# Crossbar transposes, pooled banks for the PV sums, and half of VectorE's exponent products on GpSimd, in a fused attention and feed-forward kernel

## The chip, the cores and the metric

One core of a Trainium2 chip runs the whole kernel. Times are device microseconds (us) of one execution, as the median of several; lower is better.

## The reference

```python
x = A_x                                        # (1, 2048, 512) bf16, 32 heads of 16
h  = x + attention(layernorm(x), wqkv, wo)     # softmax(q k^T / 4) v, no mask
h2 = h + (gelu(ln(h) @ w_gate) * (ln(h) @ w_up)) @ w_down     # F = 1792; returned
```

The costly part is 32 heads x 2048 x 2048 exponentials: 2048 score tiles of 128 keys by 512 queries, with one column of ones beside V so that the PV product yields the softmax's denominators too (PV: the exponentials times V). The queries are taken in five chunks of 512, 512, 512, 256 and 256 tokens.

## The kernel before

The program is laid out at build time. Small generators offer operations; a list scheduler with durations of its own puts them in a fixed order on each engine. On the chip each engine runs its order and waits on semaphores. So **how many** score tiles go to VectorE instead of ScalarE is a result of the scheduler.

TensorE writes score tiles to PSUM banks 0 to 3 for ScalarE, two at a time, and single tiles to other banks for VectorE. ScalarE's share is one instruction per pair:

```python
yield Op("act", TEXP(n), ACTF(PT[:, p0:p0 + n, :], pbank[:, b0:b0 + n, :], ACT.Exp, ...))    # 128x1024
```

VectorE's share is one conversion per tile (`dconv`, PSUM to 16-bit integers) and, for four tiles at once, two bitwise steps and a product, which split 2^x into two factors:

```python
def dchain(G):                       # X, W, E: (128, 4*512), 16 bit
    yield Op("dve", t1, ... out=W, in0=X, scalar1=0x3ff,  scalar2=0xb800, op0=bitwise_and, op1=bitwise_or)
    yield Op("dve", t1, ... out=E, in0=X, scalar1=0x7c00, scalar2=0x8,    op0=bitwise_and, op1=bitwise_or)
    yield Op("dve", t2, lambda e: e.tensor_tensor(out=X.bitcast(F16), in0=W, in1=X.bitcast(F16), op=ALU.mult), ...)
```

The PV sums of all heads gather in one bank (`PVB = 4`); when a unit of four heads by 512 queries is full it is copied out, transposed on TensorE and scaled:

```python
def ofin(u):
    yield Op("dve", 0.6, lambda e: e.tensor_copy(out=OA[:, par, :], in_=pbank[:, PVB, :]), ...)
    b = yield Acquire(...)                                   # another bank for the transposed sums
    yield Op("pe", 4 * TTR, fns=[TR(pt[:, ...], OA[:, par, ...], ident) for qt in range(4)], ...)
    ... reciprocal and the scalings, on VectorE, read from that bank
```

Padding is there to keep TensorE's clock up: where TensorE's order has a hole, the scheduler puts in a matmul of zeros, 512 columns wide (`fill_op`).

Of the kernel before, what the change touches and what calls it, by code (L numbers as in the profile page):

```python
# [165 lines left out]
ALU = mybir.AluOpType  # L166
# [694 lines left out]
class Op:  # L861
    def __init__(self, eng, dur, fns, reads=(), writes=(), gate=None, then=None, dma=None, extra=None, cols=0, port=False, mode="f"):
        self.eng, self.dur, self.cols, self.mode = eng, dur, cols, mode
        self.fns = fns if isinstance(fns, list) else [fns]
        self.reads, self.writes = list(reads), list(writes)
        self.gate, self.then, self.dma, self.extra = gate, then, dma, extra
        self.port = port or eng == "pool"


class Acquire:  # L870
    def __init__(self, reads=(), gate=None):
        self.reads, self.gate = list(reads), gate
# [15 lines left out]
class Sched:  # L888
# [5 lines left out]
    def __init__(self, P, banks):  # L894
        self.P = P
        self.t = {n: 0.0 for n in P.ENGINES}
        self.done = {}
        self.streams = []
        self.banks = [(0.0, b) for b in banks]
        self.now = 0.0  # L900
        self.fill = None
        self.debt = (0.0, 0.0)
        self.pipe = 0.0
        self.lent = set()
        self.early = True
        self.wake = None
        self.port = 0.0
        self.room = lambda: False
        self.mode = "f"
        self.due = self.INF  # L910
# [20 lines left out]
    def _rank(self, s):  # L931

        op = s.head
        if isinstance(op, Op):
            if s.fast is not None:
                return s.fast
            if op.eng == "pe" and op.writes[0] in SOFT:
                return min(s.prio, HELD[0] + s.prio * 1e-6) if self.room() else s.prio
            if op.eng == "dve" and not s.dyn and any(k in SOFT for k in op.reads):
# [3 lines left out]
    def _ready(self, op):  # L943
# [9 lines left out]
        if isinstance(op, Op):  # L953
# [5 lines left out]
            lag = SLACK if (op.eng == "pe" and op.writes[0] in SOFT) or (op.eng == "act" and op.writes[0][0] == "w") else 0.0  # L959
# [10 lines left out]
    def _emit(self, op, start):  # L970
# [7 lines left out]
        if op.eng == "pe":  # L978
            m = "r" if op.mode == "q" else op.mode
            if m != self.mode:  # L980
                start += TSW
            self.mode = m
        end = start + op.dur
        if op.port:
# [6 lines left out]
        else:  # L991
# [9 lines left out]
            self.done[tok] = end + TAIL.get(op.eng, 0.0)  # L1001
        if op.then is not None:
            op.then()

    def guard(self, cands):
# [5 lines left out]
        ok = [(r, s) for r, s in cands if s.head.mode == "q" or max(self.t["pe"], r) + s.head.dur + (TSW if s.head.mode[0] != self.mode else 0) <= due + QTOL]  # L1011
        return ok

    def run(self):
        while self.streams:
# [21 lines left out]
            for eng, cands in best.items():  # L1037
                if eng == "pe":
                    cands = self.guard(cands)
                st = max(self.t[eng], min(r for r, _ in cands))  # L1040
                lim = st + LOOK
                for r, s in cands:
                    if r <= lim:
                        st = max(self.t[eng], r)
# [22 lines left out]
            if op.eng == "pe" and self.fill:  # L1067
                f = self.fill(st, op)
                if f:
                    alt = [c for c in best["pe"] if c[1] is not s and c[0] <= f[1] + 0.05 and c[1].head.writes[0] in SOFT and c[1].head.cols >= 512]  # L1070
# [3 lines left out]
                    st, s = max(self.t["pe"], alt[0][0]), alt[0][1]  # L1074
# [9 lines left out]
SOFT = (("pb", 5), ("pb", 6), ("pb", 7))  # L1084
# [13 lines left out]
PVB = 4  # L1098
DENSE = (5, 6, 7)
# [4 lines left out]
GS = 4  # L1104
NX = 4
# [56 lines left out]
def fast_path(nc, P, base0, ARENA, pbank, flag, A_x, A_wqkv, A_wo, B_x, B_w_gate, B_w_up, B_w_down, out):  # L1162
# [20 lines left out]
    dW = at("dW", [128, GS, 512], F16)  # L1183
# [7 lines left out]
    xnT = at("xnT", [128, 4, S], BF16)  # L1191
# [4 lines left out]
    cur[0] = max(cur[0], offF + 43008)  # L1196
    dXE.append(at("dXE%d" % (NX - 1), [128, 2, GS, 512], U16, offE + 14336))
# [14 lines left out]
    hnT_c = [at("hnT_c%d" % c, [128, 4, CHUNKS[c]], BF16, h_off[c][0] + 4096) for c in range(NC)]  # L1212
# [47 lines left out]
    C = dict(exp=0, pv=0, oa=0, ln1=0, proj=0, oproj=0, gut=0, down=0, act=0, gopen=None, gk=0, gw=0, cdone=0, pvu=0, pvleft=0, gpv=0, acons=0, qpos=0, dnext=0.0, made=0)  # L1260
    otok_n = {}

# [49 lines left out]
    def masks():  # L1312
# [5 lines left out]
        yield Op("dve", 0.5, lambda e: e.memset(pbank[:, PVB, :], 0.0), writes=[("pb", PVB)])  # L1318
# [53 lines left out]

    def ln1_T(c, t):
        b = yield Acquire(reads=[("xn", t % 8), "ident"])
# [4 lines left out]
        o_ap, i_ap = xnT[:, :, 128 * t:128 * t + 128], pt[:, 0:512].rearrange("p (c s) -> p c s", c=4)  # L1379
# [5 lines left out]
    def proj_kq(items):  # L1385
        for (which, j, c, dl) in items:
# [4 lines left out]
            for hf in range(2):  # L1391
                yield Op("pe", 2 * TMM, cols=1024, fns=[MM(pbank[:, b, :], wqkv_sb[:, dc, base + 128 * j:base + 128 * j + 128], xnT[:, dc, 512 * c:512 * c + 512], dc == 0, dc == 3)
# [16 lines left out]
    def q_evac(j, c, b, dl):  # L1409

        for par in range(2):
# [8 lines left out]
    def proj_v():  # L1420
        for t in range(NT):
# [3 lines left out]
            for hf in range(2):  # L1425
                yield Op("pe", 2 * TMM, cols=1024, fns=[MM(pbank[:, b, :], xnT[:, dc, 128 * t:128 * t + 128], wqkv_sb[:, dc, 2 * D:3 * D], dc == 0, dc == 3)
# [39 lines left out]
    def qk():  # L1466
        nxt, an = 0, 0
        while nxt < len(TILES):
# [15 lines left out]
            yield Op("pe", TST * repeats([TILES[i][2] for i, _ in put]), mode="q", cols=128 * len(put), fns=fns, reads=rd, writes=[("pb", b) for _, b in put],  # L1484
# [14 lines left out]
    def close_group():  # L1499
        G = C["gopen"]  # L1500
        C["gopen"] = None
        if G["t"]:
            groups.setdefault(G["u"], []).append(G)
            sch.add(dchain(G), 70000).dyn = lambda: -4 if G["u"] == C["pvu"] and C["pvleft"] <= 5 else 70000
# [24 lines left out]
    def dget():  # L1529

        def room():
            if C["gopen"] or C["proj"] < DFROM or C["gw"] + 1 < C["gk"] or C["gk"] - C["gpv"] >= (NX if C["ln1"] == NT else NX - 1) or sch.t["dve"] > sch.now + 0.8:
# [5 lines left out]
        while True:  # L1538
            yield Wait(lambda: "qkdone" in C or room())
            if "qkdone" in C:  # L1540
                return
            G = C["gopen"] = dict(u=None, t=[], g=set(), k=C["gk"], conv=0)
            C["gk"] += 1
            C["dnext"] = sch.now + DGAP
            while len(G["t"]) < GS:
                if pick(G) is None:
                    if "qkdone" in C or (G["t"] and over(G)):
                        break
                    yield Wait(lambda: "qkdone" in C or pick(G) is not None or (G["t"] and over(G)))
                    continue  # L1550
                b = yield Acquire(gate=lambda: "qkdone" in C or over(G) or pick(G) is not None)
                i = pick(G)
                if i is None:
                    sch.release(b)
                    continue
                own[i] = ("d", G["k"])
                fns, rd = scores([(i, b)])
                wk = sch.wake | {TILES[i][2]}
                yield Op("pe", TDQ if TILES[i][2] not in sch.wake else TST, mode="r", cols=128, fns=fns, reads=rd, writes=[("pb", b)])
# [3 lines left out]
                G["g"].add(TILES[i][2])  # L1563
            close_group()

    def over(G):

        return bool(G["t"]) and unit0[G["u"] + 1] - C["qpos"] <= GLAST

    def pick(G):  # L1570
# [4 lines left out]
        if not G["t"]:  # L1575
            G["u"] = None
            u = unit_of(nxt)
            if unit0[u + 1] - nxt < ATAIL:
                u += 1
            if u < NU and qk_ready(u):  # L1580
                G["u"] = u
        u = G["u"]
        if u is None or not sch.wake or over(G):
            return None
        i0 = max(nxt, unit0[u])
        cand = [i for i in range(i0, min(unit0[u + 1], i0 + AWIN)) if i not in own and TILES[i][2] not in G["g"] | sch.wake]
        return cand[0] if cand else None

    def dconv(G, j, b):
        yield Op("dve", 0.603, lambda e: e.tensor_scalar(out=dXE[G["k"] % NX][:, 0, j, :], in0=pbank[:, b, :], scalar1=XMIN + 1024.0 * CENTER, scalar2=XMIN, op0=ALU.add, op1=ALU.max),  # L1590
                 reads=[("pb", b)], writes=[("dX", G["k"] % NX, j)], gate=lambda: C["gpv"] >= G["k"] - NX + 1 and (G["k"] % NX < NX - 1 or C["ln1"] == NT), extra=dE if G["k"] % NX == NX - 1 else None)
        sch.release(b)
        G["conv"] += 1

    def dchain(G):



        x, n = G["k"] % NX, len(G["t"])
        X, W, E = dXE[x][:, 0, 0:n, :], dW[:, 0:n, :], dXE[x][:, 1, 0:n, :]  # L1600
        kX, kW, kE = [("dX", x, j) for j in range(n)], ["dW"], [("dE", x)]
        t1, t2 = 0.07 + 0.133 * n, 0.066 + 0.267 * n
        yield Wait(lambda: G["conv"] == n)
# [3 lines left out]
        yield Op("dve", t2, lambda e: e.tensor_tensor(out=X.bitcast(F16), in0=W, in1=X.bitcast(F16), op=ALU.mult), reads=kW + kX, writes=kX, port=True)  # L1607
        G["done"] = 1

    def pv():  # L1610
        n = 0
        count = {}

        def total(u, g):
            return len(units[u][1]) * sum(2 if own[unit0[u] + 4 * kt + g][0] == "d" else 1 for kt in range(NT))

        def prod(i, tiles, last):

            u, kt, g = TILES[i]
            c, slots = units[u]  # L1620
            nq = CHUNKS[c]
            out = []
            for e, slot in enumerate(slots):
                for tl in tiles:
                    out.append((len(out), MM(pbank[32 * g:32 * g + 17, PVB, e * nq:e * nq + nq], VA[:, kt, head(slot, g), :], tl[:, e * nq:e * nq + nq],
                                             (u, g) not in count, last and count.get((u, g), 0) + 1 == total(u, g), (0, 32 * g))))
                    count[u, g] = count.get((u, g), 0) + 1
            return out

        for u in range(NU):  # L1630
            c, slots = units[u]
            r = len(slots)
            for m in range(0, NT, PVM):
                C["pvu"], C["pvleft"] = u, NT - m
                last = m + PVM >= NT
                ts = list(range(4 * n, 4 * (n + PVM)))
                yield Wait(lambda: all(i in own and (own[i][0] == "d" or i in made) for i in ts) and
                           (not last or ((not C["gopen"] or C["gopen"]["u"] != u or not C["gopen"]["t"]) and all("done" in G for G in groups.get(u, ())))))
                for G in groups.get(u, ()):
# [314 lines left out]
```

## Time and profile before

| | before |
|---|---|
| time, median of 3 | 845.17 us (844.28 to 845.54) |
| first exponential of ScalarE begins | 17.0 us |
| last one ends | 807.4 us |
| from there to the end (the tail) | 35.8 us |
| pairs of tiles on ScalarE | 796, busy 742.3 us |
| tiles on VectorE | 456, in 115 groups |

ScalarE's stage runs from its first exponential to its last. The lines behind the table, and the sum that they make, are in the prediction. The span is from the first to the last instruction; the time is some 2 us longer.

### The profile page before, as it was taken

What the parts mean: (1) busy time and instruction counts of PE and PEld (TensorE: products, weight loads), DVE (VectorE), ACT (ScalarE), POOL (GpSimd) and SP (SyncE); (2) the same over time, 40 slices, a digit from 0 to 9 for tenths busy, and PEclk for the clock granted to TensorE, in tenths of its full rate; (3) what the DMA queues carried; (4) which work ended last, traced back from release to release, by engine and by line L of the source; (5) the groups of instructions that cost most, each with busy time, mean ns of one, the idle gap of its engine ahead of it and who ended that gap; (6) DMA issues with size and microseconds to landing.
All of it is one profiled execution on the core that took longest, in us unless ns stands there. A gap on an engine that the chain in (4) does not pass through costs nothing.

```text
span 843.2 us, 16693 instructions
## 1 busy us (share of the span) xinstructions
PE 819.5 (97%) x6773; PEld 254.4 (30%) x6773; DVE 769.0 (91%) x1246; ACT 786.3 (93%) x833; POOL 42.9 (5%) x100
## 2 busy tenths in 40 slices
PE   8999999999999999999999989999999989999997
PEld 3222222222222222222222222222233333333455
DVE  7569999999999999999989989999999999899862
ACT  3979999999999999999999999999999999999941
POOL 5600000000010000000010000000010000000000
PEclk9999999999999999999999999999999999999999
DMA  6000004300000000000000000000000000000000
GB/s 200 1 1 1 1 2 160 116 1 1 8 7 1 2 1 2 7 26 7 2 14 1 1 1 2 7 26 7 2 21 7 2 1 2 2 26 14 2 13 18
DMA packets 12327, 15.06 MB, mean 18 GB/s; under 512 B 1744, under 2 KB 11216, under 8 KB 12240
## 3 DMA queue, kind: packets, MB, share of 16 engines
q1 hardware_dynamic: 12240, 13.90, 5.0%
q8 instruction: 55, 0.90, 0.4%
q14 instruction: 32, 0.26, 0.1%
HBM read 11.80 MB, written 2.10 MB: 16 GB/s over the span
## 4 chain that ended last, share of the span: by engine, by line
PE 75%; ACT 12%; DVE 6%; issue 5%; POOL 1%; ACTq 0%; POOLq 0%; DVEq 0%
PE pbank L1272 46%; PE pbank L1271 21%; ACT PT L1278 11%; PE pbank L1870 3%; DVE dXE L1590 2%; DVE dXE L1607 1%; PE pbank L1275 1%; ACT GUT L1809 1%; PE pbank L1867 1%; PE pbank L1880 1%; DVE dXE L1605 1%; POOL xn_sb L1369 1%; DVE dW L1604 1%; PE pbank L1725 0%; PE pbank L1747 0%
## 5 line engine op out<-in xcount | busy, mean ns | idle before, releaser
L1278 ACT ACTIVATE PT<-pbank 128x1024 bf16<-128x1024 f32 x796 | 742.3, 1072 | 17.7 <-PE pbank L1272 14.6
L1272 PE MATMUL pbank<-QT,KT 32*128 32x512 bf16 x2048 | 345.0, 384 | 7.2 <-ACT PT L1278 4.9
L1590 DVE TENSOR_SCALAR dXE<-pbank 128x512 uint16<-128x512 f32 x456 | 296.9, 682 | 15.9 <-PE pbank L1272 12.8
L1272 PEld LDWEIGHTS pbank<-QT,KT 32*128 32x128 bf16 x2048 | 84.2, 91 | 311.5 <-ACT PT L1278 220.8
L1272 PE MATMUL pbank<-PT,VA 128*17 128x512 bf16 (+1 forms) x1992 | 149.4, 339 | 0.1
L1607 DVE TENSOR_TENSOR dXE<-dW,dXE 128x2048 f16<-128x2048 f16 (+1 forms) x115 | 139.1, 1210 | 2.0
L1604 DVE TENSOR_SCALAR dW<-dXE 128x2048 uint16<-128x2048 uint16 (+1 forms) x115 | 78.1, 679 | 0.8
L1605 DVE TENSOR_SCALAR dXE<-dXE 128x2048 uint16<-128x2048 uint16 (+1 forms) x115 | 78.1, 679 | 0.0
L1272 PE MATMUL pbank<-dXE,VA 128*17 128x512 f16 (+1 forms) x1136 | 70.3, 339 | 0.0
L1271 PE MATMUL pbank<-hnT_c,wu_sb 128*128 128x512 bf16 (+1 forms) x280 | 59.7, 346 | 7.4 <-DVE GUT L1823 6.8
L1271 PE MATMUL pbank<-hnT_c,wg_sb 128*128 128x512 bf16 (+1 forms) x280 | 65.5, 340 | 0.0
L1271 PE MATMUL pbank<-wd_sb,GUT 128*128 128x512 bf16 x224 | 59.2, 382 | 0.0
L1272 PEld LDWEIGHTS pbank<-PT,VA 128*17 128x17 bf16 x1992 | 39.2, 88 | 65.3 <-issue 57.8
L1870 PE MATMUL pbank<-ones_bf,zero_bf 128*128 128x512 bf16 x168 | 55.7, 386 | 0.0
L1823 DVE TENSOR_TENSOR GUT<-pbank,GUT 128x512 bf16<-128x512 f32 x56 | 37.3, 685 | 16.0 <-PE pbank L1271 12.8
L1741 POOL TENSOR_SCALAR rstd<-mv 128x1 f32<-128x1 f32 x16 | 6.6, 413 | 761.0 <-DVE mv L1739 761.0
L1271 PE MATMUL pbank<-xnT,wqkv_sb 128*128 128x512 bf16 x128 | 37.8, 383 | 0.0
L1271 PEld LDWEIGHTS pbank<-hnT_c,wu_sb 128*128 128x128 bf16 x280 | 23.5, 99 | 32.5 <-issue 11.8
L1797 DVE CAST GUT<-pbank 128x512 bf16<-128x512 f32 x49 | 33.1, 680 | 0.0
L1271 PEld LDWEIGHTS pbank<-hnT_c,wg_sb 128*128 128x128 bf16 x280 | 19.5, 97 | 27.8 <-issue 20.6
L1272 PEld LDWEIGHTS pbank<-dXE,VA 128*17 128x17 bf16 x1136 | 18.7, 88 | 29.8 <-issue 24.0
L1271 PEld LDWEIGHTS pbank<-wd_sb,GUT 128*128 128x128 bf16 x224 | 17.0, 97 | 27.0 <-issue 14.3
(82 smaller groups left out, 390.8 us busy)
## 6 DMA issues: line engine op xcount, KB each, us to landing
xres<-in_A_x_dram SPq DMA_DIRECT2D x16, 128.0 KB, 2.2
out_dram<-out_sb SPq DMA_DIRECT2D x16, 128.0 KB, 1.7
wg_sb<-in_B_w_gate_dram SPq DMA_DIRECT2D x1, 1792.0 KB, 7.1
wu_sb<-in_B_w_up_dram SPq DMA_DIRECT2D x1, 1792.0 KB, 11.2
wd_sb<-in_B_w_down_dram SPq DMA_DIRECT2D x1, 1792.0 KB, 17.4
x_sb<-in_A_x_dram SPq DMA_DIRECT2D x3, 512.0 KB, 8.3
wqkv_sb<-in_A_wqkv_dram SPq DMA_DIRECT2D x1, 896.0 KB, 7.5
x_sb<-in_A_x_dram SPq DMA_DIRECT2D x2, 256.0 KB, 2.9
```

The source lines that it names most:

```text
L1271: return lambda e: e.matmul(o, l, r, start=start, stop=stop)
L1272: return lambda e: e.matmul(o, l, r, start=start, stop=stop, tile_position=tile)
L1275: return lambda e: e.transpose(out=o, in_=i, identity=idn)
L1278: return lambda e: e.activation(out=o, in_=i, func=func, **kw)
L1369: lambda e: e.tensor_scalar(out=xn_sb[:, t % 8, :], in0=x_sb[:, t, :], scalar1=rstd[:, tt_], scalar2=htmp[:, tt_], op0=ALU.mult, op1=ALU.add),
L1590: yield Op("dve", 0.603, lambda e: e.tensor_scalar(out=dXE[G["k"] % NX][:, 0, j, :], in0=pbank[:, b, :], scalar1=XMIN + 1024.0 * CENTER, s ...
L1604: yield Op("dve", t1, lambda e: e.tensor_scalar(out=W.bitcast(U16), in0=X, scalar1=0x3ff, scalar2=0xb800, op0=ALU.bitwise_and, op1=ALU.bit ...
L1605: yield Op("dve", t1, lambda e: e.tensor_scalar(out=E, in0=X, scalar1=0x7c00, scalar2=0x8, op0=ALU.bitwise_and, op1=ALU.bitwise_or), reads ...
L1607: yield Op("dve", t2, lambda e: e.tensor_tensor(out=X.bitcast(F16), in0=W, in1=X.bitcast(F16), op=ALU.mult), reads=kW + kX, writes=kX, por ...
L1797: yield Op("dve", 0.6, lambda e: e.tensor_copy(out=o_ap, in_=i_ap), reads=[("pb", b)], writes=keys, extra=dE)
L1823: yield Op("dve", 0.6, lambda e: e.tensor_tensor(out=o_ap, in0=u_ap, in1=o_ap, op=ALU.mult), reads=[("pb", b)] + keys, writes=keys)
L1870: fill_op = Op("pe", TMM, lambda e: e.matmul(pbank[:, PVB, :], zero_bf[:], ones_bf[:], start=False, stop=False, skip_group_check=True), re ...
```

## The change

Its intent is to take work from VectorE (evictions, which are copies out of PSUM, of transposes; half of the products), so that it can take more tiles from ScalarE. A crossbar transpose is a DMA (`dma_start_transpose`), so it needs neither TensorE nor an eviction. Cut to its core, in the order of the title (a second buffer for `dW`, the scheduler's new rules and bookkeeping and its new constants are left out):

```diff
 def ln1_T(c, t):                       # half of the 16 normalised input tiles
+    if c >= TURN_X:
+        yield turn(xnT[:, t, :, :], xn_sb[:, t % 8, :], ...)     # Op("sp", ... e.dma_start_transpose(out=o, in_=i) ...)
+        ...
+        return
 ...
 def ofin(u):
-    ... out=OA[:, par, :], in_=pbank[:, PVB, :]
+    ... out=OA[:, par, :], in_=pbank[:, pvbank[u], :]
+    sch.release(pvbank[u])
+    if turned:                           # 31 of 32 units
+        yield turn(OAT[par], OA[:, par, :], ...)             # crossbar; then the scalings go to GpSimd
 ...
 def post(c, qt):                       # all chunks but the last
-    ... 4 transposes on TensorE and a copy, twice (OnT, hnT)
+    yield turn(OnT[:, qt, :, :], Otok[:, cp, qt, :], ...)
+    yield turn(hT[:, qt, :, :], hn_sb[:, qt, :], ...)
 ...
-PVB = 4
-DENSE = (5, 6, 7)
+DENSE = (4, 5, 6, 7)                   # the PV sums take any free bank of these
+NPOOL = 2
 ...
 def dchain(G):                         # a group is now a whole key row of four tiles
-    yield Op("dve", t2, ... product of 4 tiles)
+    yield Op("dve", t2, ... product of tiles 0 to nd-1)      # nd = 4 - NPOOL
+    for j in range(nd, n):
+        yield Op("pool", TPOOL, lambda e, j=j: e.tensor_tensor(out=X[:, j, :], in0=W[:, j, :], in1=X[:, j, :], op=ALU.mult), ...)
 ...
 def q_evac(j, c, b, dl):               # scaling of Q: one plain copy on VectorE, two scalings on GpSimd
```

## The prediction

> **What bounds the kernel now.** The kernel runs attention (32 heads, 2048 queries by 2048 keys, so 2048 score tiles of 128x512) and a GELU feed-forward on one core. Exponentials of score tiles are shared: ScalarE takes them in pairs (128x1024 per instruction), VectorE takes the rest by bit arithmetic (one conversion per tile, then two bitwise steps and a product for four tiles at once). I read first the groups of instructions by cost, to see who does how much:
>
> ```profile
> L1278 ACT ACTIVATE PT<-pbank 128x1024 bf16<-128x1024 f32 x796 | 742.3, 1072 | 17.7 <-PE pbank L1272 14.6
> L1590 DVE TENSOR_SCALAR dXE<-pbank 128x512 uint16<-128x512 f32 x456 | 296.9, 682 | 15.9 <-PE pbank L1272 12.8
> L1607 DVE TENSOR_TENSOR dXE<-dW,dXE 128x2048 f16<-128x2048 f16 (+1 forms) x115 | 139.1, 1210 | 2.0
> L1604 DVE TENSOR_SCALAR dW<-dXE 128x2048 uint16<-128x2048 uint16 (+1 forms) x115 | 78.1, 679 | 0.8
> L1870 PE MATMUL pbank<-ones_bf,zero_bf 128*128 128x512 bf16 x168 | 55.7, 386 | 0.0
> ```
>
> 796 pairs are 1592 tiles on ScalarE and 456 on VectorE, 2048 together. The last row is padding: 168 matmuls of zeros that only keep TensorE's clock up. So TensorE has room although the page shows it 97% busy. Next the busy time by stretches of the span, to find where which engine is full:
>
> ```profile
> 100.00:200.00 100.00, 97.73 (x758) 25.25 (x751) 98.95 (x152) 99.33 (x109) 0.00 (x0) 1.00 0.17 59
> 300.00:400.00 100.00, 98.00 (x737) 26.38 (x736) 97.27 (x151) 98.84 (x101) 0.00 (x0) 1.00 0.03 9
> 800.00:843.00 43.00, 36.14 (x289) 23.18 (x286) 19.78 (x37) 14.26 (x18) 1.58 (x4) 0.99 0.05 15
> ```
>
> Columns: length, then busy time of TensorE, its weight loads, VectorE, ScalarE, GpSimd, then granted clock. From 100 us to 800 us three engines are all at 96 to 100%, GpSimd is empty. Which of the three sets the pace is told by the table of waits:
>
> ```profile
> PEld pbank L1272 <- ACT PT L1278: 221.0, 546, 1.0
> PEld pbank L1272 <- DVE dXE L1590: 18.3, 50, 0.5
> ACT PT L1278 <- PE pbank L1272: 14.6, 27, 2.9
> ```
>
> TensorE's weight loads wait 221 us for ScalarE to free its score banks and only 18.3 us for VectorE's conversions; ScalarE waits 14.6 us for TensorE. ScalarE is the pacemaker, with almost no gaps. Its timeline and that of the end of the kernel:
>
> ```profile
> 17.00 1.02 ACT L1278 ACTIVATE PT<-pbank 128x1024 bf16<-128x1024 f32 x1 [2.08 <-PE pbank L1272]
> 62.37 19.87 ACT L1278 ACTIVATE PT<-pbank 128x1024 bf16<-128x1024 f32 x21 [2.86 <-PE pbank L1272]
> 136.92 165.50 ACT L1278 ACTIVATE PT<-pbank 128x1024 bf16<-128x1024 f32 x179 [0.20 <-PE pbank L1272]
> ...
> 803.66 3.77 ACT L1278 ACTIVATE PT<-pbank 128x1024 bf16<-128x1024 f32 x4
> 819.42 6.29 PE L1271 MATMUL pbank<-hnT_c,wg_sb 128*128 128x256 bf16 x56
> 825.54 6.28 PE L1271 MATMUL pbank<-hnT_c,wu_sb 128*128 128x256 bf16 x56
> 831.84 6.22 PE L1271 MATMUL pbank<-wd_sb,GUT 128*128 128x512 bf16 x28
> ```
>
> Exponentials run from 17.0 us to 803.66 + 3.77 = 807.4 us. Then a tail of 843.2 - 807.4 = 35.8 us follows: the last query chunk's projection and its whole feed-forward. So span = start (17.0) + ScalarE's stage (790.4) + tail (35.8).
>
> **What the Trainium skill says.** "ScalarE: Activation LUTs", section "What ACT_TABLE_LOAD costs": 186 ns + 0.833 ns per element, and back-to-back instructions overlap by about 93 ns. For 1024 elements that is 1039 - 93 = 946 ns; the trace has 1072 ns alone and 165.5/179 = 925 ns in a row, so a pair costs what its row's busy time says, 742.3/796 = 0.9325 us. "SBUF — State Buffer", section "Who interferes with whom": GpSimd shares a port pair with VectorE as an exclusive lock, which VectorE's fast one-input modes and its two-input SBUF operations take. The trace of before, with GpSimd empty, can't show it. "GPSIMD Engine Reference", section 3.1: about 2.6 cycles per element for two inputs at 1.2 GHz; not shown before either. "VectorE: DVE Perf Modes", section "The three transpose paths": 1309 ns for one 128x128 crossbar transpose, against 390 ns on TensorE; the kernel before has none on the crossbar.
>
> **The change part by part.** Counts of after are from its instruction order, which is fixed at build.
>
> VectorE loses: 8 of 16 copies of xnT (419 ns each, 3.4 us); the two scaled Q evictions become one plain copy (22.9 us to about 15 x 0.68 + 0.7 = 10.9, so 12.0); 38 of 40 output scalings (14.1 us, so 13.5); 28 of 30 copies of OnT and hnT (11.9 us, so 11.1); products of 2048 columns (139.1 us) become 119 of 1024 columns (693 ns, the time of the one such product in before: 82.5, so 56.6). It gains 20 conversions (456 to 476, 296.9/456 = 0.65 us each: 13.0) and four more groups' bitwise steps (119 x 2 x 0.684 - 156.2 = 6.6). Net -77 us: 769 to about 692 us, 82% of the span. This lies beside ScalarE and is worth nothing by itself; it counts only by the tiles it lets VectorE take.
>
> GpSimd gains 238 products of 512 columns, an estimate of 512 x 2.6 / 1.2 = 1.11 us each from the skill's figure, 264 us, plus about 45 us of Q and output scalings. With VectorE's bitwise steps (163 us) and products (82 us) the shared port would be asked for about 264 + 45 + 43 + 163 + 82 = 600 us of 840: it fits, with some blocking.
>
> TensorE loses 268 of 320 transposes; padding grows from 203 (168 + 35 of another form) to 247 matmuls, so the builder of the order found more holes, not fewer. No gain on the path by itself.
>
> ScalarE: the tiles it keeps are what counts. 476 tiles on VectorE instead of 456 leave 786 pairs instead of 796: 10 x 0.9325 = -9.3 us. The 77 us freed are thus hardly spent: a tile costs VectorE (296.9 + 139.1 + 2 x 78.1)/456 = 1.3 us before, so they would have paid for some 59. Also the GELU of the fourth chunk with its two table loads (2 x 1.28 + 3.3 = 5.9 us) no longer splits the exponentials; it comes after the last of them.
>
> Tail: this is the price. After the last exponential the order of before had 8 up matmuls and 28 down matmuls of chunk four left; the order of after has 20 gate, 56 up and 28 down. From before's timeline (6.29/56 = 0.112 us per 256-column matmul, 0.222 per down matmul): PV 0.6 + 0.6, gates 2.25, ups 6.3, downs 6.2, transposes 0.4 + 0.6 + 0.8, output projection 1.9, then the last chunk 6.29 + 6.28 + 0.16 + 6.22 = 38.6 us of TensorE, plus some 2 us in which ups wait for the late GELU, plus 5.1 us from the last matmul to the end as before (838.1 to 843.2). That is 45.8 us against 35.8: +10.
>
> Start: the first pair should come at about 17 us again (24 against 26 projection matmuls ahead of it). Of ScalarE's 17.7 us of gaps 9.5 lie before 62.4 us, behind TensorE (the timeline's gaps added up); 32 transposes fewer (1.8 us) help, crossbar latency for the second half of xnT hurts. I take -2 us.
>
> Sum on the path: -9.3 - 5.9 + 10 - 2 = -7.2 us, so 845.2 - 7.2 = 838.
>
> **Rivals.** (1) Stalls of the fixed order. Every engine runs in order, and TensorE's PV matmuls of a group now wait for VectorE, then GpSimd, under a port lock. If each of 119 groups comes 0.2 to 0.4 us later than the order assumes and ScalarE has no spare scores, that is +24 to +48 us: 862 to 886. For it: ScalarE's gaps are near zero, so any TensorE stall shows; the gaps can only grow. Against it: VectorE gets 18% of slack, TensorE has padding, and before's equally fixed order leaves ScalarE only 8.2 us of gaps after the start-up. (2) The freed engines close ScalarE's gaps: 786 x 0.925 = 727, GELUs inside 26.5, idle 8, start 17, tail 44, and the 2 us between span and measured time make 825. For it: VectorE at 97 to 99% must cause some of the gaps. Against: only 8.2 us of them lie after the start-up. (3) Crossbar latency. VectorE's reciprocal, in order, waits for 31 of the 67 transposes, TensorE for others, all on one queue. If each is exposed for 1 us, VectorE has the room (150 us), and perhaps 10 us reach ScalarE: 848.
>
> **Range and chances.** The -9.3 and -5.9 are counted, the tail is firm to 2 us, the start to 3; ScalarE's idle time in the middle is open, more upward than downward. Predicted 838, range 827 to 853. Faster by over 2% means under 828.3, which needs rival 2 in full: 0.13. Slower by over 2% means over 862.1, which needs rival 1: 0.10. Within 2%: 0.77.
>
> **What would show it.** Right: 786 pairs at 0.93 us, waits for ScalarE still the largest of TensorE's, VectorE near 82%, the last pair ending near 790 us and a tail of 44 to 47 us. Wrong: ScalarE idle well over 18 us between 62 us and its last pair, with TensorE's PV rows waiting for GpSimd (rival 1); a tail under 40 us; GpSimd products far from 1.1 us; VectorE's bitwise steps much longer than 684 ns, which would be the lock; transposes landing after over 4 us.

## The result, and the profile after

Ratios here are the mean time of one kernel's fast runs over that of the other's of the same rounds, so not quite the ratio of the medians quoted.

The changed kernel took 840.18 us (837.67 to 841.18, 4 runs), the one before 844.72 us beside it (844.25 to 845.54, 4 runs): ratio 0.994, 95% interval 0.9924 to 0.9957. That is 4.5 us faster, within 2%.

| | before | predicted | after |
|---|---|---|---|
| time, us | 845.17 | 838 | 840.18 |
| first exponential, us | 17.0 | 15 | 17.1 |
| ScalarE's stage, us | 790.4 | 775.2 | 777.2 |
| tail, us | 35.8 | 45.8 | 44.5 |
| pairs on ScalarE | 796 | 786 | 786 |
| VectorE busy, us | 769 | 692 | 734.4 |

The groups of the changed kernel (line, engine, operation, output and input, count, then busy us and mean ns, then the engine's idle time ahead of them and what ended it):

```profile
L1312 ACT ACTIVATE PT<-pbank 128x1024 bf16<-128x1024 f32 x786 | 732.4, 1063 | 20.5 <-PE pbank L1306 17.6
L1656 POOL TENSOR_TENSOR dXE<-dW,dXE 128x512 f16<-128x512 f16 x238 | 303.4, 1295 | 317.7 <-DVE dXE L1654 317.7
L1636 DVE TENSOR_SCALAR dXE<-pbank 128x512 uint16<-128x512 f32 x476 | 308.4, 685 | 38.4 <-PE pbank L1306 36.3
L1651 DVE TENSOR_SCALAR dXE<-dXE 128x2048 uint16<-128x2048 uint16 x119 | 103.9, 873 | 0.0
L1654 DVE TENSOR_TENSOR dXE<-dW,dXE 128x1024 f16<-128x1024 f16 x119 | 90.7, 762 | 2.3
L1650 DVE TENSOR_SCALAR dW<-dXE 128x2048 uint16<-128x2048 uint16 x119 | 90.7, 762 | 0.1
```

The two bitwise steps took 679 ns each before. Now they take 762 and 873 ns, with the same operands: GpSimd works beside them. A mean hides how. Shortest, median and longest (ns, after the count) of GpSimd's products, of the second bitwise step and of the conversions:

```profile
L1656 POOL TENSOR_TENSOR dXE<-dW,dXE x238: 1144/1156/1723, 64.5 to 794.4; 128x512 f16<-128x512 f16 x119
L1651 DVE TENSOR_SCALAR dXE<-dXE x119: 674/687/1648, 61.3 to 790.8; 128x2048 uint16<-128x2048 uint16 x119
L1636 DVE TENSOR_SCALAR dXE<-pbank x476: 657/684/694, 48.1 to 781.5; 128x512 uint16<-128x512 f32 x159
```

Half of these bitwise steps take about what they took alone (687 ns or less, against 679) and some take more than twice that; likewise half of GpSimd's products take 1156 ns or less. The conversions, which read PSUM, never stretch. So single instructions collide; it is not a general slowing.

The stretches that answer to those shown of before (length; busy time of TensorE, its weight loads, VectorE, ScalarE, GpSimd; clock):

```profile
100.00:200.00 100.00, 95.10 (x730) 24.13 (x737) 89.66 (x135) 99.72 (x109) 66.26 (x61) 1.00 0.19 64
300.00:400.00 100.00, 95.93 (x718) 26.63 (x725) 93.49 (x149) 96.99 (x99) 46.12 (x38) 1.00 0.05 14
```

GpSimd is half busy, VectorE has some air, ScalarE is still at 97 to 100%. TensorE's 95% is not air to the same extent: this trace holds 6491 matmuls to 6572 weight loads, so about 80 matmul records are missing. The waits:

```profile
PEld pbank L1306 <- ACT PT L1312: 223.2, 569, 0.8
PEld pbank L1306 <- DVE dXE L1636: 42.7, 124, 1.1
ACT PT L1312 <- PE pbank L1306: 17.6, 30, 2.3
```

TensorE still waits mostly for ScalarE, but its waits for VectorE's conversions have grown from 18.3 to 42.7 us. The start, the last exponentials and the tail in the timeline:

```profile
17.11 1.02 ACT L1312 ACTIVATE PT<-pbank 128x1024 bf16<-128x1024 f32 x1 [2.31 <-PE pbank L1306]
...
763.48 30.86 ACT L1312 ACTIVATE PT<-pbank 128x1024 bf16<-128x1024 f32 x33 [0.17 <-PE pbank L1306]
...
795.76 1.68 ACT L1895 ACTIVATE GUT<-GUT 128x1792 bf16<-128x1792 bf16 x1
...
814.10 6.28 PE L1305 MATMUL pbank<-hnT_c,wg_sb 128*128 128x256 bf16 x56
820.21 6.28 PE L1305 MATMUL pbank<-hnT_c,wu_sb 128*128 128x256 bf16 x56
826.74 5.99 PE L1305 MATMUL pbank<-wd_sb,GUT 128*128 128x512 bf16 x27 [0.16 <-issue]
```

The last exponential ends at 763.48 + 30.86 = 794.3 us. The fourth chunk's GELU, which used to split the exponentials, comes after them, and the tail is 838.8 - 794.3 = 44.5 us. The crossbar, in the list of transfers (the last number is us from issue to landing):

```profile
OAT<-OA SPq DMA_TRANSPOSE x31, 2.5
OnT<-Otok SPq DMA_TRANSPOSE x14, 2.5
hnT_c<-OnT SPq DMA_TRANSPOSE x14, 2.5
xnT<-xn_sb SPq DMA_TRANSPOSE x8, 2.4
```

### The profile page after: what moved, and what is told of

It reads as the page before. It is cut to its first block, busy times and chain, and to the rows that moved or that the text cites. A ratio compares the mean times of both kernels' runs of the same rounds, so it can differ in the third digit from the quotient of the medians.

```text
span 838.8 us, 16702 instructions
## 1 busy us (share of the span) xinstructions
PE 796.0 (95%) x6491; PEld 245.4 (29%) x6572; DVE 734.4 (88%) x1189; ACT 773.9 (92%) x821; POOL 398.8 (48%) x406
## 4 chain that ended last, share of the span: by engine, by line
PE 54%; ACT 18%; DVE 13%; issue 7%; POOL 3%; DMA 1%; ACTq 0%; POOLq 0%; DVEq 0%
PE pbank L1306 33%; PE pbank L1305 19%; ACT PT L1312 17%; DVE dXE L1636 5%; POOL dXE L1656 2%; DVE dXE L1651 2%; PE pbank L1959 2%; DVE dW L1650 1%; DVE dXE L1654 1%; ACT GUT L1895 1%; DVE OA L1741 1%; DMA xnT<-xn_sb 1%; POOL xn_sb L1403 1%; DVE GUT L1909 1%; DVE GUT L1882 0%
## 5 line engine op out<-in xcount | busy, mean ns | idle before, releaser
L1312 ACT ACTIVATE PT<-pbank 128x1024 bf16<-128x1024 f32 x786 | 732.4, 1063 | 20.5 <-PE pbank L1306 17.6
L1656 POOL TENSOR_TENSOR dXE<-dW,dXE 128x512 f16<-128x512 f16 x238 | 303.4, 1295 | 317.7 <-DVE dXE L1654 317.7
L1306 PE MATMUL pbank<-QT,KT 32*128 32x512 bf16 x2048 | 356.6, 384 | 17.3 <-ACT PT L1312 10.9
L1636 DVE TENSOR_SCALAR dXE<-pbank 128x512 uint16<-128x512 f32 x476 | 308.4, 685 | 38.4 <-PE pbank L1306 36.3
L1306 PE MATMUL pbank<-PT,VA 128*17 128x512 bf16 (+1 forms) x1968 | 128.5, 339 | 0.3 <-issue 0.3
L1651 DVE TENSOR_SCALAR dXE<-dXE 128x2048 uint16<-128x2048 uint16 x119 | 103.9, 873 | 0.0
L1654 DVE TENSOR_TENSOR dXE<-dW,dXE 128x1024 f16<-128x1024 f16 x119 | 90.7, 762 | 2.3
L1650 DVE TENSOR_SCALAR dW<-dXE 128x2048 uint16<-128x2048 uint16 x119 | 90.7, 762 | 0.1
L1306 PEld LDWEIGHTS pbank<-PT,VA 128*17 128x17 bf16 x1968 | 34.6, 88 | 62.3 <-issue 57.9
L1458 POOL TENSOR_SCALAR QT<-QT,qmask 128x512 bf16<-128x512 bf16 x30 | 26.8, 897 | 27.3 <-DVE QT L1455 26.2
L1305 PEld LDWEIGHTS pbank<-hnT_c,wu_sb 128*128 128x128 bf16 x280 | 24.0, 99 | 29.4 <-issue 10.3
L1763 POOL TENSOR_TENSOR Otok<-OAT,LINV 128x256 bf16<-128x256 bf16 (+1 forms) x38 | 29.4, 781 | 3.1 <-DVE LINV L1757 3.0
## 6 DMA issues: line engine op xcount, KB each, us to landing
wd_sb<-in_B_w_down_dram SPq DMA_DIRECT2D x1, 1792.0 KB, 17.1
```

The lines of the kernel that those rows point to most:

```text
L1305: return lambda e: e.matmul(o, l, r, start=start, stop=stop)
L1306: return lambda e: e.matmul(o, l, r, start=start, stop=stop, tile_position=tile)
L1312: return lambda e: e.activation(out=o, in_=i, func=func, **kw)
L1636: yield Op("dve", 0.603, lambda e: e.tensor_scalar(out=dXE[G["k"] % NX][:, 0, j, :], in0=pbank[:, b, :], scalar1=XMIN + 1024.0 * CENTER, s ...
L1650: yield Op("dve", t1, lambda e: e.tensor_scalar(out=W.bitcast(U16), in0=X, scalar1=0x3ff, scalar2=0xb800, op0=ALU.bitwise_and, op1=ALU.bit ...
L1651: yield Op("dve", t1, lambda e: e.tensor_scalar(out=E, in0=X, scalar1=0x7c00, scalar2=0x8, op0=ALU.bitwise_and, op1=ALU.bitwise_or), reads ...
```

## The experiments

Twelve kernels ran, three rounds each, beside the kernel before on the same chip, which took 844.6 to 845.3 us there (7 runs each time). Two kinds are mixed. In the first, the order of instructions stays exactly that of the changed kernel (of the kernel before in e4) and one kind of instruction is made shorter (the result is then wrong): this asks what a resource is worth. In the second, a part of the change is undone and the scheduler lays out a new order: this asks what a part is worth, with the scheduler's reaction in it.

The theory to begin with (A) was the prediction's: ScalarE alone sets the pace, and the lock between GpSimd and VectorE costs little. The rival (V): GpSimd's products and the slowed VectorE stand right behind ScalarE.

**e1 and e2: the products made short.**

```diff
-tensor_tensor(out=X[:, j, :], in0=W[:, j, :], in1=X[:, j, :])               # GpSimd, e1 and e2
+tensor_tensor(out=X[:, j, 0:16], in0=W[:, j, 0:16], in1=X[:, j, 0:16])
-tensor_tensor(out=X[:, 0:nd, :], in0=W[:, 0:nd, :], in1=X[:, 0:nd, :])      # VectorE, e2 only
+tensor_tensor(out=X[:, 0:nd, 0:16], in0=W[:, 0:nd, 0:16], in1=X[:, 0:nd, 0:16])
```

> Same order as the changed kernel, but the GpSimd products take 16 of 512 columns (wrong result on purpose), so that GpSimd's time and its port lock nearly vanish. Theory A (ScalarE's stage plus tail; GpSimd costs only part of the extra gaps, 14.2 us after the start-up against 8.2 before): VectorE busy falls from 734 to about 695 us, the time by 4 to 8 us to 832 to 836. Rival R (late GpSimd products and the lock hold up the fixed order by over 12 us): below 828. Rival N (nothing of it on the path): 839 to 841.

> As e1, and VectorE's own products of 1024 columns cut to 2 x 16 too (wrong result on purpose, same order): VectorE loses about 70 us more. Theory A: VectorE is not the pacemaker, so at most 2 us below e1. Rival V (VectorE shares the pace): 8 us or more below e1.

e1 took 834.84 us (834.05 to 835.88; ratio to before 0.988, 0.9863 to 0.9896), e2 835.14 us (833.24 to 835.39; 0.9888, 0.9871 to 0.9904). Three groups of e1:

```profile
L1654 DVE TENSOR_TENSOR dXE<-dW,dXE 128x1024 f16<-128x1024 f16 x119 | 85.1, 715 | 2.3
L1651 DVE TENSOR_SCALAR dXE<-dXE 128x2048 uint16<-128x2048 uint16 x119 | 82.6, 694 | 0.0
L1656 POOL TENSOR_TENSOR dXE<-dW,dXE 128x16 f16<-128x16 f16 x238 | 75.9, 338 | 501.9 <-DVE dXE L1654 501.9
```

With GpSimd short, VectorE's bitwise steps are back at 689 and 694 ns: the slowing was GpSimd's doing. It costs VectorE 734.4 - 701.7 = 33 us of busy time, but the kernel only 5 us, with GpSimd's own lateness in it. Taking a further 62 us of products from VectorE (e2) brings nothing more. So far theory A.

**e3 and e4: ScalarE's exponentials made shorter.** 480 of 512 columns of each tile, in the changed kernel (e3) and in the one before (e4); the columns left out are set once to ones.

```diff
-ACTF(PT[:, p0:p0 + n, :], pbank[:, b0:b0 + n, :], ACT.Exp, ...)
+ACTF(PT[:, p0:p0 + n, 0:480], pbank[:, b0:b0 + n, 0:480], ACT.Exp, ...)
```

> Same order as the changed kernel, but each exponential of ScalarE takes 2 x 480 instead of 2 x 512 columns (wrong result on purpose; the rest of the tiles is set to 1 at the start): 64 x 0.833 ns = 53 ns less for each of 786, 42 us in all. Theory A (ScalarE sets the pace, VectorE at 88% and TensorE with padding have room): 20 to 40 us shorter, 800 to 820. Rival V (VectorE or TensorE set it as much): less than 10 us shorter, over 830.

> The same shortening in the kernel before (796 x 53 ns = 42 us). There VectorE is at 97 to 99% through the middle stage. Theory A: ScalarE sets the pace but VectorE is right behind, so the gain is smaller than in e3: 5 to 20 us, 825 to 840; the difference to e3 is the VectorE time that the change freed and did not spend. Rival: the same gain as in e3, then the freed VectorE time was no room at all.

e3 took 833.21 us (829.53 to 836.01; 0.9868, 0.9831 to 0.9906), e4 838.93 us (838.08 to 839.58; 0.9932, 0.9916 to 0.9949). The exponentials of e3:

```profile
L1312 ACT ACTIVATE PT<-pbank 128x960 bf16<-128x960 f32 x786 | 701.0, 980 | 42.5 <-PE pbank L1306 34.6
```

They are busy 701.0 us in place of 732.4, 31 us less, which is 40 ns for each and not the 53 expected. (The 0.833 ns per column of the expectation is the figure of "ScalarE: Activation LUTs", section "What ACT_TABLE_LOAD costs", that the prediction cites; the GELUs of the trace of before agree, (3182 - 1688)/1792 = 0.834 ns.) The kernel gained 7 us; most of the rest went into waits for TensorE, 34.6 us in place of 17.6. e3's runs spread with the clock, from 829.53 us at 0.999 to 836.01 at 0.989; against the changed kernel's run at 0.999 (837.67) the gain is 8. In e4 it gained 5.7. That is in the range of theory A for e4, but so close to e3 that its rival reads it better: the VectorE time that the change freed was no room here. Theory A, as far as it said that only ScalarE matters, fell: in both kernels something stands within 7 us behind it. I then took TensorE for it, since its order alternates score and PV matmuls in step with ScalarE, and tested that.

**e5 and e6: ScalarE and the products short at once; then the padding narrow too.**

```diff
 e5: the edits of e2 and e3 together
 e6: the same, and in both padding matmuls
-matmul(pbank[:, b, :], zero_bf, ones_bf, ...)
+matmul(pbank[:, b, 0:16], zero_bf, ones_bf[:, 0:16], ...)
```

> Order of the changed kernel kept; exps 2x480 columns AND all products (VectorE's and GpSimd's) 16 columns, wrong on purpose. ScalarE relieved by about 31 us and VectorE by up to 110 us at once. If TensorE's fixed order is balanced right behind ScalarE (the theory after e3_act480): 828 to 833 us, at most about 4 us below e3_act480, and ScalarE's idle time stays above 35 us, most of it ended by TensorE. Rival (VectorE stood behind ScalarE in e3_act480, its multiplied tiles reaching TensorE late): below 815 us.

> As e5_act480_prod16, and the 247 padding matmuls write 16 columns in place of 512, which takes some 247 x 0.2 = 50 us of work from TensorE in the same order. If TensorE is what stands behind ScalarE and its granted clock stays near 1.0: 795 to 815 us. If the padding only fills waits of TensorE: within 4 us of e5_act480_prod16. If the clock falls without the padding: about the same or slower, with a mean granted clock clearly below 0.997.

e5 took 815.62 us (815.24 to 816.45; 0.9656, 0.964 to 0.9672). My theory of TensorE (828 to 833) is refuted; the rival's "below 815" was missed by 0.6 us, but its direction holds. The four kernels with one order make a table:

| median us | products full | products 16 columns |
|---|---|---|
| exponentials full | 840.2 | 835.1 |
| exponentials 480 columns | 833.2 | 815.6 |

Short products are worth 5.1 us while ScalarE is full and 17.6 us once it is relieved; shorter exponentials are worth 7 us while the products are full and 19.5 us without them. That is the sign of two limits side by side: **ScalarE, and right behind it the lane of VectorE and GpSimd.** Which of these two e5 cannot say, as it shortens both. In e5 the stretch from 300 to 400 us shows what is next:

```profile
300.00:400.00 100.00, 98.40 (x747) 27.44 (x745) 85.27 (x154) 95.64 (x102) 12.65 (x36) 1.00 0.06 16
```

VectorE is down to 85% and TensorE at 98% (no records are missing here), part of it padding. Whether TensorE is the third limit e6 could not tell: it took 884.42 us (883.21 to 884.77; 1.0464, 1.0447 to 1.0481), because its mean granted clock was 0.844. Its expectation named that outcome.

**e7: only the padding narrow.** The edit of e6 alone on the changed kernel; the result stays right.

> The changed kernel with only the padding matmuls narrowed to 16 columns (result stays right, order the same). If ScalarE and TensorE are balanced, relief of TensorE alone is worth at most the 14 us that ScalarE idles after start-up: 830 to 840 us, if the clock stays. If TensorE alone set the time: below 825 us. If the padding holds the granted clock up: slower than the changed kernel, with a lower mean clock.

917.08 us (893.6 to 917.56), 53 to 77 us slower than the changed kernel, at a mean clock of 0.862 in the fastest run and 0.826 in the other three, as the third branch of its expectation said. The lower clock here is the effect under test: all eight runs of e6 and e7 have it (0.862 or less), and no run of e5, e8 and the kernel before, which ran beside them on the same chip (0.996 or more). Its page:

```profile
PE 878.4 (96%) x6572; PEld 250.3 (27%) x6572; DVE 738.9 (81%) x1189; ACT 787.5 (86%) x821; POOL 399.0 (44%) x406
...
PEclk9999997755555599999656599999657589999999
...
L1312 ACT ACTIVATE PT<-pbank 128x1024 bf16<-128x1024 f32 x786 | 746.0, 1044 | 84.4 <-PE pbank L1306 80.6
```

The second line is the granted clock in tenths, over 40 slices: it falls to half for long stretches. TensorE still runs as many instructions and is "96% busy"; only the width of its 247 padding matmuls is gone. ScalarE now waits 80.6 us for TensorE, against 17.6. The padding is not waste.

**e8: the crossbar part undone.** All 67 crossbar transposes go back to TensorE, with an eviction each; pooled banks and GpSimd products stay.

```diff
-TURN_X = 2
+TURN_X = 4
-turned = C["ln1"] == NT and u < NU - 1
+turned = False
-if c < NC - 1:       # twice, in post
+if False:
```

> The changed kernel with all 67 crossbar transposes put back on TensorE with an eviction each (the scheduler lays the order out anew; right result). If the crossbar part brought the gain of the change by freeing VectorE and TensorE: 845 to 860 us. If transposes could be hidden anyway where they are (in the idle of TensorE's padding and VectorE's 12%): 838 to 843 us, like the changed kernel.

835.73 us (835.62 to 837.2; 0.989, 0.9874 to 0.9907): 4.5 us **faster** than the full change, outside both expectations. Its groups:

```profile
L1312 ACT ACTIVATE PT<-pbank 128x1024 bf16<-128x1024 f32 x778 | 728.0, 1059 | 20.7 <-PE pbank L1306 17.6
L1636 DVE TENSOR_SCALAR dXE<-pbank 128x512 uint16<-128x512 f32 x492 | 321.5, 684 | 23.6 <-PE pbank L1306 21.4
L1651 DVE TENSOR_SCALAR dXE<-dXE 128x2048 uint16<-128x2048 uint16 x123 | 94.6, 769 | 0.0
L1650 DVE TENSOR_SCALAR dW<-dXE 128x2048 uint16<-128x2048 uint16 x123 | 88.5, 720 | 0.0
```

The scheduler gave VectorE 123 groups in place of 119, so ScalarE has 8 pairs fewer. That is where its gain lies: the exponentials are 4.4 us shorter, while ScalarE's gaps within its stage are the same (18.5 us, against 18.3). The bitwise steps are also stretched less (720 and 769 ns). GpSimd no longer scales the PV sums there (in the changed kernel 38 instructions of 781 ns, 29.4 us, where VectorE needs 14.3 us for the 40 of them in e8); that this is the reason is not shown. So the crossbar part takes evictions from VectorE and TensorE, and yet at these settings the order made with it is the worse one. Why the scheduler then places four groups fewer I did not find out.

**e9 and e10: GpSimd's products undone, with and without the crossbar.**

```diff
-NPOOL = 2
+NPOOL = 0            # e9; e10 with the edit of e8 as well
```

> The changed kernel with all four products of a group back on VectorE (the scheduler lays the order out anew; right result): no lock between VectorE and GpSimd, but some 0.4 us more VectorE work per group (1.21 us in place of 0.76, less 0.2 us of ands back at 684 ns). If the GpSimd half is what paid for the change: 846 to 865 us. If it is worth nothing net: 838 to 843 us.

> Crossbar and GpSimd products both undone: only the pooled PV banks and the exps in whole key rows are left (right result). If crossbar and GpSimd products each cost or bring the same whatever the other does, this is e9_npool0 less the 4.5 us that e8_pe_turn came out below the changed kernel. If the crossbar pays only where VectorE is full (no GpSimd half): 3 us or more above e9_npool0. If the pooled banks alone are the gain: below 840 us.

e9 gave a **wrong result** (relative error 0.98); its 884.81 us (883.98 to 885.77) is not used. e10 was right: 849.89 us (847.88 to 850.07; 1.0051, 1.0034 to 1.0068). Its "less the 4.5 us" could not be judged without e9; that the pooled banks alone are the gain (below 840) is refuted. Without e9, one path from the kernel before to the changed one is measured, always with the scheduler's new order:

| kernel | time, us | pairs on ScalarE | ScalarE's stage, us | tail, us |
|---|---|---|---|---|
| before | 844.8 | 796 | 790.4 | 35.8 |
| + pooled banks and whole key rows (e10) | 849.9 | 794 | 789.7 | 41.1 |
| + half of the products on GpSimd (e8) | 835.7 | 778 | 773.0 | 46.2 |
| + crossbar: the change | 840.2 | 786 | 777.2 | 44.5 |

The row of e10 also has the scaling of Q on GpSimd, the second `dW` buffer and the new rules and constants of the scheduler, which come with all three. The products on GpSimd bring 14 us; the pooled banks, with all that comes with them, cost 5 (all of it in the tail: 41.1 - 35.8 = 5.3), and the crossbar part costs 4.5. These are prices with the order that the scheduler happened to make: e11 shows that another order moves more than the two small ones.

**e11: other settings, to beat both.** One product of four on GpSimd in place of two, and the scheduler's constants chosen anew among several hundred tried in its own model, of which only the order was taken.

```diff
-NPOOL = 2;  TPOOL = 1.11;  DB = 1;  KEND = 2;  SLACK = 0.3
+NPOOL = 1;  TPOOL = 1.3;   DB = 0;  KEND = 1;  SLACK = 0.1
-DGAP = 3.0;  DBUSY = 2.0;  LOOK = 0.12;  ATAIL = 8;   DFROM = 20
+DGAP = 4;    DBUSY = 1;    LOOK = 0.06;  ATAIL = 12;  DFROM = 10
```

> A candidate to beat both: the changed kernel with one of four products on GpSimd in place of two, and the scheduler's own settings chosen anew (774 exps of ScalarE in place of 786, 125 key-row groups on VectorE in place of 119; right result). From the changed kernel: 12 pairs fewer x 0.93 us = 11 us off ScalarE, 6 groups x (4 x 0.685 + 2 x 0.75 + about 1.1) = 32 us more VectorE. If ScalarE's count sets the time as long as VectorE stays under about 92%: 826 to 832 us. If VectorE or the fixed order takes it back, as e5_act480_prod16 hints: 836 to 845 us.

The result is right, and it took **818.37 us** (817.63 to 818.69; 0.9683, 0.9667 to 0.9699), 3.2% faster than before and better than either expectation:

```profile
L1312 ACT ACTIVATE PT<-pbank 128x1024 bf16<-128x1024 f32 x774 | 722.2, 1065 | 12.6 <-PE pbank L1306 9.5
L1636 DVE TENSOR_SCALAR dXE<-pbank 128x512 uint16<-128x512 f32 x500 | 323.0, 683 | 13.4 <-PE pbank L1306 12.2
L1656 POOL TENSOR_TENSOR dXE<-dW,dXE 128x512 f16<-128x512 f16 x125 | 165.4, 1324 | 414.1 <-DVE dXE L1654 414.1
L1651 DVE TENSOR_SCALAR dXE<-dXE 128x2048 uint16<-128x2048 uint16 x125 | 89.4, 715 | 0.0
```

Against the changed kernel the span falls by 838.8 - 816.7 = 22.1 us: exponentials 732.4 - 722.2 = 10.2; ScalarE's gaps within its stage 18.3 - 10.1 = 8.2 (added up from the trace's records); tail 44.5 - 40.4 = 4.1. Together 22.5, of which a start later by 0.3 takes some back. VectorE is busier than in the changed kernel (754.3 us, 92%) and yet delivers in time (TensorE waits 30.2 us for its conversions, against 42.7). Its bitwise steps are stretched less (714 and 715 ns), with half the products on GpSimd (165 us in place of 303). The half alone does not do it: e12 below has as much on GpSimd (161 us), and there they take 702 and 812 ns. What falls together in time counts too, and that the order decides.

**e12: is it the GpSimd share alone?**

```diff
-NPOOL = 2
+NPOOL = 1            # nothing else
```

> The changed kernel with one product of four on GpSimd in place of two and no other setting touched (the scheduler lays the order out anew; 776 exps of ScalarE in place of 786, 124 groups in place of 119; right result). If two products on GpSimd were too many (they slow VectorE's own 16-bit passes by the lock and deliver late), this alone gives most of what e11_tune1 gave: ScalarE 10 x 0.933 = 9 us less, its gaps down from 14 towards 5 us: 818 to 828 us. If the other settings of e11_tune1 made its gain: 834 to 842 us.

Again a **wrong result** (relative error 0.496), and times in two clusters: 829.69 us at a mean clock of 1.0 in the profiled run, 837.78 to 842.1 us at 0.98 in the other four (median of all five 840.48; ratio 0.9939, 0.9915 to 0.9963). It does not settle what the smaller share is worth. Executing the programs of e9 and e12 off the chip gives the same relative errors, with whole chunks of query tokens wrong (the first two in e12, the first four in e9) and the rest right. So the orders themselves are at fault, not a race on the chip; the scheduler's rules for reusing some buffer do not cover these orders. Which buffer I did not find. Both have the crossbar part and another GpSimd share than the changed kernel, but so has e11, which is right; the changed kernel, e8 and e10 are right too.

## Why the prediction was right, step by step

**The sum was right, term by term.** It put the span together from start, ScalarE's stage and tail. The stage was predicted as 790.4 - 9.3 - 5.9 = 775.2 us and measured as 777.2. The ten pairs gave 742.3 - 732.4 = 9.9 us (predicted 9.3), and the two table loads and the GELU that left the stage gave the 5.9 in full (GELUs and table loads within the stage: 32.4 us before, 26.5 after). Against that the gaps within the stage, added up from the trace's records, grew from 15.8 to 18.3 us. The tail was predicted at 45.8 and measured at 44.5. Only the 2 us at the start did not come: 17.1 us, not 15. The sum had no term for the gaps. That they changed by no more than 2.5 us was derived from nothing, and there the number was lucky: with other orders or lengths they are 10.1 (e11) or 40.4 us (e3).

**VectorE was mis-sized.** 692 us was predicted, 734.4 measured. The term that failed is "119 x 2 x 0.684" for the bitwise steps and 693 ns for the product: measured were 762 + 873 ns and 762 ns, so (78 + 189 + 69) x 119 = 40 us of the 42. The prediction had named the lock ("it fits, with some blocking") without a size. e1 shows the cause and the price: 33 us of VectorE, 5 us of the kernel. Two of the prediction's own signs thus failed: VectorE is at 88% and not near 82%, and "bitwise steps much longer than 684 ns", a sign of being wrong, came. The time hardly noticed.

**GpSimd's product** was estimated at 1.11 us and took 1.295 us in the mean, but 1.156 in the median: the estimate was near for a product that collides with nothing.

**Two readings of the trace of before were loose.** VectorE was not at 96 to 100% all the way from 100 to 800 us: from 500 to 600 us it was at 93.9%, and from 700 to 780 us busy 75.05 of 80. And 1072 ns is not an exponential "alone" but the mean record of overlapping ones; the lone first one took 1.02 us. The sum uses neither.

**Rival 1** (stalls of the fixed order, 862 or more) did not come: TensorE's PV matmuls waited just 2.9 us for GpSimd, and their weight loads 3.5. **Rival 3** (crossbar latency) did not come either: transposes landed after 2.4 to 2.5 us and the waits for them are under 2 us in all. **Rival 2** (the gaps closed) did not come with this order; e11's order closed part of them.

**What the prediction got right for too simple a reason.** "ScalarE is the pacemaker, with almost no gaps" is true, and it suggests that a shorter ScalarE is a shorter kernel. e3 and e4 contradict that: 31 and 29 us off ScalarE gave 7 and 5.7 us, and e5 shows that the next limit is VectorE with GpSimd. The prediction's "18% of slack" on VectorE could not be spent in this order: its tiles must be ready when TensorE's order asks for them, and at 88% busy it was already late at times (42.7 us of TensorE's waits). It is the order more than the share that decides this, as e11 with VectorE at 92% shows. And "TensorE has room", because part of its work is padding, holds only as long as something else keeps its clock up (e7).

**Where the change's gain went.** GpSimd's half brings 14 us; pooled banks and what comes with them cost 5 of that in the tail, and the crossbar part 4.5 through a worse split, all with the orders that the scheduler made. What stays open: why the order with crossbar gives VectorE fewer groups, how much of e11's gain is its smaller GpSimd share and how much the other settings (e12 could not say), whether VectorE or GpSimd is the second limit, and what stands behind both limits of e5.

## What to carry to other kernels

Before crediting a helper engine, cost its lock: work moved to GpSimd came back as 33 us on VectorE, and half as much moved, under a better order, was part of the fastest version here. Read such a cost from shortest, median and longest, not from the mean: they tell collisions from a general slowing. Where two engines are both near full, shorten each alone and then both in a fixed order: the table of four tells two limits side by side from one, which waits and busy shares could not. And before removing padding, look at the clock it holds up: here it filled 78 us of TensorE's time (the 231 of one of its two forms, in e5) and narrowing it cost 53 to 77 us.

## What the Trainium skill lacked or had wrong

- "GPSIMD Engine Reference", section 3.1: from its 2.6 cycles per element the prediction estimated 1.11 us for a 128x512 product of two f16 inputs. The median of 238 was 1156 ns and, in e1, 218 ns for 16 columns. From these two an estimate is (1156 - 218)/496 = 1.89 ns per column and some 190 ns for each instruction; the section has no number for such a fixed part. The mean was 1295 ns, by collisions with VectorE.
- "SBUF — State Buffer", section "Who interferes with whom": the runs fit the lock (half of the steps untouched, some more than doubled, the conversions out of PSUM never), but the page has no size for it in mixed work. Here 128x2048 bitwise steps went from 679 to 762 and 873 ns with GpSimd 48% busy, to 714 and 715 ns with GpSimd 32% busy (e11), but 702 and 812 at 31% (e12), and back to 689 and 694 ns with GpSimd at 20% (e1). So GpSimd's share alone does not give the size.
- "VectorE: DVE Perf Modes", section "The three transpose paths": it has 1309 ns for one 128x128 tile on the crossbar; for several squares in one issue it has no number. One issue of a 128x512 tile, four such squares, landed after 2.4 to 2.5 us here, less than twice that.
- "TensorE: Matmul & The Clock Gate", Part 1: activity holds the clock up, and a low clock did come in long stretches at half; but the page does not say what share of a window counts as busy, or that the width of matmuls counts in it. With the same 6572 matmuls, TensorE 96% busy by the profile and no gap between matmuls over 2.2 us (2.1 in the changed kernel), narrowing the padding from 512 to 16 columns let the mean clock fall from 0.997 to 0.826 (e7).
